# Products of 1024 columns from double banks, one ring for ScalarE's banks, and output chains that share a bank with the sums

## The chip, the cores and the metric

The kernel runs on one core of a Trainium2 chip. The metric is device microseconds of the whole program, median of several executions; executions of one kernel mostly agree within 0.7%. An execution that is more than 1.5% above the fastest of its kernel counts as slow, the others as fast. Each kernel was run beside executions of the kernel before on the same chip; the medians of those lie between 771.1 and 775.0 us, so that times of different rounds can be set side by side to about 4 us, and 1 to 3 us between them are not to be read closely. "Slot" below is one step of the kernel's steady loop. "Clock" is TensorE's granted clock as the profile records it, 1.0 for full and 0.5 for half.

## The reference

Two parts, joined. The first pools x (4 batches of 12416 tokens of 128 channels) into 32 inducing vectors h by softmax attention, then lets each token attend to the 32 h. The second is a gated layer with 1536 hidden units:

```python
def mab(q, kv):
    s = scale * (q @ kv.transpose(0, 2, 1))
    s = s - s.max(-1, keepdims=True)
    a = np.exp(s)
    a /= a.sum(-1, keepdims=True) + 1e-09
    return a @ kv
h = mab(I, x)                     # I: the inducing vectors, per batch
x1 = mab(x, h)                    # per token, over 32 h
...
gate = np.maximum(x1 @ w_gate, 0.0)
val = x1 @ w_val
return (gate * val @ w_out)
```

## The kernel before

The second attention is never formed. Its unnormalised weights p2 (32 rows per token block) are multiplied straight with hgv = h @ w_gate and h @ w_val, so each hidden block needs only matmuls with 32 rows (K = 32), and the squared softmax sum (z2) is divided out at the end. A pair of token blocks (2 x 512 tokens) takes twelve slots, one for each 128 of the 1536 hidden units:

```python
for k in range(2):                 # TensorE, slot `at`
    if k < len(unit):
        form(unit[k], 0)           # g_k of this slot, into a g bank (ring of 3)
    if k < len(before):
        form(before[k], 1)         # v_k of the slot before, into a v bank (ring of 3)
...                                # planned ScalarE/VectorE/DMA work of other parts
for _ in range(steps.pop(at, 0)):
    out_step(at)                   # output chain: o += wo[i] x gv[i], 12 steps, one o bank
for f in fill.pop(at, []):
    f()                            # s2, z2, s1T, hgv, h ... into one "m" bank
for t in unit:
    nc.scalar.activation(out=g16, in_=t["ps", 0], func=AF.Relu)
for t in before:
    nc.vector.tensor_tensor(out=t["dst"], in0=t["g16"], in1=t["ps", 1], op=ALU.mult)
```

(Allocation of g16 is cut. s2 and z2 are the scores and the softmax sums of the second attention, s1T the scores of the first.) The four forms of a slot are placed on four different row groups of the array and run together: in the kernel before three of them start at 112.38 us and the fourth at 112.51, each 0.37 to 0.39 us long. A chain of twelve 128x128x512 matmuls per token block follows, planned as

```python
plan_chain(base + 10 + 6 * k, (2, 2, 2, 3, 3), ...)
```

that is 2, 2, 2, 3, 3 steps in five slots and one slot of pause, in which ScalarE empties the o bank. The kernel's eight PSUM banks are g 3, v 3, m 1, o 1.

The softmax here doesn't subtract the row's maximum and nothing guards it: scores larger than these inputs give would overflow.

Of the kernel before, what the change touches and what calls it, by code (L numbers as in the profile page):

```python
# [17 lines left out]
def kernel(  # L18
# [39 lines left out]
    def bank(tag, name, shape=None, dtype=FP32):  # L58
        return psum.tile(
            shape or [P, BLK], dtype, tag=tag, bufs=3 if tag in ("g", "v") else 1, name=name  # L60
        )
# [61 lines left out]
    def new_xT(q):  # L123
        t0, t1 = crange(q)
        return st([P, t1 - t0, P], FP16, "xT" if t1 - t0 == CT else "xTr", 10 if t1 - t0 == CT else 2)
# [14 lines left out]
    def hgv_pe(hT, k, tag="m"):  # L140
        ps = bank(tag, "hgv_ps")
        for r in range(4):
            nc.tensor.matmul(
                ps[32 * r : 32 * r + 32, :],
                hT[:, 0:M],
                (wg if r % 2 == 0 else wv)[:, k * BLK : (k + 1) * BLK],
                start=True,
                stop=True,
            )
        return ps  # L150

    def hgv_evac(hgv, ps, k):
        if k % 2 == 0:
            nc.scalar.copy(out=hgv[:, k * BLK : (k + 1) * BLK], in_=ps)
        else:
            nc.vector.tensor_copy(out=hgv[:, k * BLK : (k + 1) * BLK], in_=ps)
# [5 lines left out]
    def s2_pe(hT, xT, pr):  # L162
        ps = bank("m", "s2_ps")
# [10 lines left out]
    def s2_exp(ps, pr):  # L174
        p2 = st([P, BLK], FP16, "p2", 3)
        if pr < NPAIR:
            nc.scalar.activation(out=p2, in_=ps, func=AF.Exp, scale=sm_scale)  # L177
        else:
            nc.scalar.activation(out=p2[0:64, 0:P], in_=ps[0:64, 0:P], func=AF.Exp, scale=sm_scale)
        return p2  # L180

    def z2_pe(p2, pr):
        ps = bank("m", "z2_ps", [P, TPB, 2], FP32)
        if pr < NPAIR:
            for t in range(TPB):
                nc.tensor.matmul(ps[:, t, :], p2[:, t * P : (t + 1) * P], sel, start=True, stop=True)  # L186
        else:
            nc.tensor.matmul(ps[:, 0, 0:1], p2[0:64, 0:P], sel[0:64, 0:1], start=True, stop=True)
        return ps

    def z2_recip(ps, pr):
        z2i = st([P, TPB, 2], FP32, "z2i", 4)
        if pr < NPAIR:
            nc.vector.reciprocal(out=z2i, in_=ps)
        else:
            nc.vector.reciprocal(out=z2i[:, 0, 0:1], in_=ps[:, 0, 0:1])
        return z2i
# [5 lines left out]
    hT_ps = bank("o", "hT_ps", [P, M], FP32)  # L203
    z1_ps = bank("m", "z1_ps", [P, CT, M], FP32)
# [17 lines left out]
    for q in range(NCH):  # L222
# [16 lines left out]
        for a in range(t0, t1, 8):  # L239
            e = min(a + 8, t1)  # L240
            ps = bank("g" if a == t0 else "v", "xT_ps", [P, 8, P], FP16)
# [10 lines left out]
        ps = bank("g" if q % 2 else "v", "s1_ps", [P, CT, M], FP32)  # L252
# [11 lines left out]
    pss = [hgv_pe(hT, k, "g") for k in range(3)]  # L264
# [28 lines left out]
    def ev_z2(b, pr, at):  # L293
        def pe():
            ps = z2_pe(p2s[(b, pr)], pr)

            def dve():
                z2is[(b, pr)] = z2_recip(ps, pr)

            post[at + 1].append(dve)  # L300

        fill[at].append(pe)

    for b in range(B):
        for pr in range(NPAIR + 1):
            if (b, pr) == (0, 0):
                ev_z2(0, 0, 1)
            elif pr == 0:
                base = slot(b - 1, NPAIR - 1, 0)
                ev_s2(b, 0, base + 9)  # L310
                ev_z2(b, 0, base + 12)
            else:
                base = slot(b, pr - 1, 0)
                ev_s2(b, pr, base + 3)
                ev_z2(b, pr, base + 6)


    def plan_phase1(b):
# [11 lines left out]
        for q in range(NCH):  # L330
# [17 lines left out]
            at = at0 + NFF * q  # L348
# [4 lines left out]
            def s1(q=q, at=at + 21):  # L353
                ps = bank("m", "s1T_ps")
# [25 lines left out]
            if q < NQ:  # L380
                fill[at + 21].append(s1)

        at = at0 + NFF * NCH + 9

        def s1_rest(at=at):
            ps = bank("m", "s1T_ps")
# [23 lines left out]
        at = at0 + NFF * (NQ + 2) + 8  # L410

        def h_part(q):
            if q == 0:
                s["h_ps"] = bank("m", "h_ps", [P, P], FP32)
# [16 lines left out]
        for q, d in enumerate((0, 1, 1, 2, 3, 4, 5)):  # L431
            fill[at + d].append(lambda q=q: h_part(q))

        def sums():
# [8 lines left out]
        post[at + 6].append(sums)  # L443

        def join():
            ps = bank("m", "hz_ps", [P, 2, M], FP32)
# [3 lines left out]
            def dve():  # L450
                s["hT"] = finish_h(ps[:, 0, :], ps[:, 1, :])
                s["hgv"] = new_hgv()

            post[at + 13].append(dve)

        fill[at + 12].append(join)
        for k in range(3):

            def mk(k=k, a=at + 13 + 2 * k):
                ps = hgv_pe(s["hT"], k)  # L460
                post[a + 1].append(lambda: hgv_evac(s["hgv"], ps, k))

            fill[at + 13 + 2 * k].append(mk)
# [5 lines left out]
    chains = []  # L469

    def out_step(at):

        c = chains[0]
        i = c["i"]
        w = c["w"]
        if i == 0:
            c["ps"] = bank("o", "o_ps")
        nc.tensor.matmul(  # L478
            c["ps"][:, 0:w], wo[:, i, :], c["gv"](i), start=(i == 0), stop=(i == NFF - 1)
        )  # L480
        c["i"] += 1
        if c["i"] < NFF:
            return
        chains.pop(0)
        ps, nt = c["ps"], w // P

        def evac():
            oT = st([P, BLK], FP16, "oT", 3)
            nc.scalar.copy(out=oT[:, 0:w], in_=ps[:, 0:w])  # L489

            def tr():
# [3 lines left out]
                def scale():  # L495
                    osb = st([P, TPB, P], FP32, "osb", 3)
                    z = z2is[c["key"]]
                    for t in range(nt):
                        zz = z[:, t, c["k"] : c["k"] + 1]
# [9 lines left out]
                    def store():  # L509
                        nc.sync.dma_start(  # L510
                            out=ov[c["b"]][:, c["t0"] : c["t0"] + nt, :], in_=osb[:, 0:nt, :]
                        )

                    post[at + 5].append(store)

                post[at + 3].append(scale)

            post[at + 2].append(tr)

        post[at + 1].append(evac)  # L520

    steps = defaultdict(int)

    def plan_chain(first, counts, **c):
        chains.append(dict(i=0, **c))
        for d, n in enumerate(counts):
            steps[first + d] += n
# [3 lines left out]
    def units():  # L531
        for b in range(B):
            for pr in range(NPAIR + 1):
                base = slot(b, pr, 0)
                p2, hgv = p2s[(b, pr)], state[b]["hgv"]
                if pr < NPAIR:
                    gvs = [st([P, NFF, BLK], FP16, "gv", 5) for _ in range(2)]
                    for k in range(2):
                        plan_chain(
                            base + 10 + 6 * k,  # L540
                            (2, 2, 2, 3, 3),
                            w=BLK,
                            gv=(lambda i, g=gvs[k]: g[:, i, :]),
                            key=(b, pr),
                            k=k,
                            b=b,
                            t0=(2 * pr + k) * TPB,
                        )
                    for s in range(NFF):
                        yield [  # L550
                            dict(
                                mm=[
                                    [(slice(0, BLK), s, p2[r : r + 32, :], hgv[r : r + 32, :])]
                                    for r in (64 * k, 64 * k + 32)
                                ],
                                dst=gvs[k][:, s, :],
                            )
                            for k in range(2)
                        ]
                else:  # L560
                    gv = st([P, NFF, P], FP16, "gvr", 1)
                    plan_chain(
                        base + 10,
                        (6, 6),
                        w=P,
                        gv=(lambda i, g=gv: g[:, i, :]),
                        key=(b, pr),
                        k=0,
                        b=b,
                        t0=NT - 1,  # L570
                    )
                    for s in range(3):
                        yield [
                            dict(
                                mm=[
                                    [
                                        (
                                            slice(i * P, (i + 1) * P),
                                            4 * s + i,
                                            p2[r : r + 32, 0:P],  # L580
                                            hgv[r : r + 32, :],
                                        )
                                        for i in range(4)
                                    ]
                                    for r in (0, 32)
                                ],
                                dst=gv[:, 4 * s : 4 * s + 4, :].rearrange("p i c -> p (i c)"),
                            )
                        ]

    def form(t, j):
        ps = t["ps", j] = bank("gv"[j], "gv"[j] + "_ps")
        for cols, s, p2, hgv in t["mm"][j]:
            nc.tensor.matmul(ps[:, cols], hgv[:, s * P : (s + 1) * P], p2, start=True, stop=True)  # L594

    at = 0
    todo_units = units()
    before = []
# [52 lines left out]
```

## Time and profile before

The median is 773.9 us. What matters of the profile:

| | kernel before |
|---|---|
| span of the profiled execution | 771.5 us |
| VectorE busy, 110 to 700 us | 98.9% |
| VectorE idle before its products | 7.0 us |
| ScalarE idle before its relus | 40.2 us |
| mean clock | 0.971 |

How the rows are read stands in the prediction.

### The profile page before, as it was taken

The numbers are of one execution on the slowest core, as the hardware profiler recorded it, in microseconds if no ns is written. First come the engines' busy times: TensorE is split into PE (matmuls) and PEld (weight loads), VectorE is DVE, ScalarE is ACT, GpSimd is POOL, SyncE is SP. The second block draws the span as 40 slices with busy tenths as digits, with TensorE's granted clock in tenths as the row PEclk, the third lists the DMA queues.
The fourth block names the chain that finished last, engine by engine and source line by source line (L and its number), as shares of the span: only waits on it lengthen the run. The fifth ranks groups of instructions, "written<-read, shape, count | busy, mean of one in ns | idle before, by whom it ended". The sixth has DMA issues, their size and how long they took to land.

```text
span 771.5 us, 15512 instructions
## 1 busy us (share of the span) xinstructions
PE 709.3 (92%) x4621; PEld 210.3 (27%) x4621; DVE 722.4 (94%) x1270; ACT 695.4 (90%) x1386; POOL 207.2 (27%) x418
## 2 busy tenths in 40 slices
PE   5699999999999999999999999999999999999993
PEld 4422222232232222222222222223222222222221
DVE  3399999999999999999999999999999999999991
ACT  4589999999989999999998999999989999999991
POOL 0303433221232243122123323322122212212212
PEclk9759999999999999999998999999999999999998
DMA  8635675211136756312134676421121121121122
GB/s 312 199 83 135 158 190 124 69 57 49 55 119 150 202 141 163 87 58 51 52 117 128 151 184 172 102 64 47 55 57 53 50 62 55 49 63 56 49 62 60
DMA packets 121172, 78.87 MB, mean 102 GB/s; under 512 B 102880, under 2 KB 105472, under 8 KB 118016
## 3 DMA queue, kind: packets, MB, share of 16 engines
q1 hardware_dynamic: 121088, 77.89, 37.3%
q8 instruction: 36, 0.59, 0.3%
q14 instruction: 48, 0.39, 0.2%
HBM read 27.80 MB, written 25.43 MB: 69 GB/s over the span
## 4 chain that ended last, share of the span: by engine, by line
PE 51%; ACT 20%; issue 12%; DMA 8%; DVE 4%; POOL 3%; SPq 0%; ACTq 0%; POOLq 0%; DVEq 0%
PE o_ps L478 23%; PE g_ps L594 18%; ACT g L616 14%; PE v_ps L594 7%; DMA xT<-x 3%; DVE gv L618 3%; DMA o<-oT 3%; ACT oT L489 3%; POOL osb L500 2%; ACT p L177 1%; POOL x L337 1%; ACT p1T L367 1%; PE xT_ps L243 1%; DMA p1g<-p1T 1%; PE h_ps L423 1%
## 5 line engine op out<-in xcount | busy, mean ns | idle before, releaser
L618 DVE TENSOR_TENSOR gv<-g,v_ps 128x512 f16<-128x512 f16 x1152 | 696.2, 679 | 7.0 <-PE v_ps L594 5.8
L616 ACT ACTIVATE g<-g_ps 128x512 f16<-128x512 f32 x1164 | 615.6, 626 | 40.2 <-PE g_ps L594 20.1
L594 PE MATMUL v_ps<-p,hgv 32*128 32x512 f16 (+1 forms) x1200 | 368.3, 381 | 4.7 <-DVE gv L618 2.8
L478 PE MATMUL o_ps<-gv,wo 128*128 128x512 f16 x1152 | 336.6, 389 | 0.3 <-ACT oT L489 0.3
L594 PE MATMUL g_ps<-p,hgv 32*128 32x512 f16 (+1 forms) x1200 | 303.3, 381 | 28.8 <-ACT g L616 26.5
L500 POOL TENSOR_SCALAR osb<-o,z2i 128x128 f32<-128x128 f16 x388 | 168.0, 447 | 527.6 <-DMA o<-oT 310.9
L594 PEld LDWEIGHTS <-hgv 32*128 32x128 f16 x2400 | 91.0, 91 | 287.6 <-issue 276.4
L478 PEld LDWEIGHTS <-wo 128*128 128x128 f16 x1200 | 76.9, 98 | 189.4 <-issue 164.9
L489 ACT CAST oT<-o_ps 128x512 f16<-128x512 f32 (+1 forms) x100 | 58.5, 585 | 4.4 <-PE o_ps L478 4.4
L337 POOL CAST x<-x 128x2048 f16<-128x2048 f32 x18 | 34.0, 1890 | 5.3 <-DMA x<-in_x_dram 5.3
L177 ACT ACTIVATE p<-s_ps 128x512 f16<-128x512 f32 x48 | 30.8, 641 | 2.7 <-PE s_ps L167 2.6
L167 PE MATMUL s_ps<-xT,hT 128*64 128x512 f16 x96 | 20.0, 413 | 1.6 <-DVE hT L137 1.6
L243 PE MATMUL xT_ps<-eye,x 128*128 128x128 f16 x97 | 11.1, 287 | 8.1 <-ACT x L227 4.4
L245 DVE COPY xT<-xT_ps 128x1024 f16<-128x1024 f16 x6 | 4.2, 692 | 13.7 <-PE xT_ps L243 13.7
L186 PEld LDWEIGHTS <-p 128*128 128x128 f16 x192 | 11.5, 97 | 12.4 <-issue 2.3
L247 ACT COPY xT<-xT_ps 128x1024 f16<-128x1024 f16 x6 | 6.1, 1012 | 6.4 <-PE xT_ps L243 6.4
L186 PE MATMUL z_ps<-sel,p 128*128 128x2 f16 x192 | 11.7, 165 | 0.0
L367 ACT ACTIVATE p1T<-s1T_ps 128x512 f16<-128x512 f32 x18 | 11.6, 645 | 0.0
L243 PEld LDWEIGHTS <-x 128*128 128x128 f16 x97 | 8.5, 130 | 9.4 <-ACT x L227 5.7
L167 PEld LDWEIGHTS <-hT 128*64 128x64 f16 x96 | 5.3, 107 | 20.1 <-issue 18.4
L618 DVE TENSOR_TENSOR gvr<-g,v_ps 128x512 f16<-128x512 f16 x12 | 8.1, 674 | 2.2 <-PE g_ps L594 1.2
L227 ACT CAST x<-x 128x1024 f16<-128x1024 f32 x6 | 6.2, 1038 | 4.0 <-DMA x<-in_x_dram 4.0
(74 smaller groups left out, 112.7 us busy)
## 6 DMA issues: line engine op xcount, KB each, us to landing
x<-in_x_dram SPq DMA_DIRECT2D x24, 1024.0 KB, 5.7
out_dram<-osb SPq DMA_DIRECT2D x96, 256.0 KB, 2.0
o<-oT SPq DMA_TRANSPOSE x100, 2.4
x<-in_moe_w_gate_dram SPq DMA_DIRECT2D x1, 768.0 KB, 4.3
x<-in_moe_w_val_dram SPq DMA_DIRECT2D x1, 768.0 KB, 4.3
x<-in_moe_w_out_dram SPq DMA_DIRECT2D x1, 768.0 KB, 6.1
xT<-x SPq DMA_TRANSPOSE x18, 4.3
p1g<-p1T SPq DMA_TRANSPOSE x18, 2.9
```

What stands on the lines that cost most here:

```text
L167: nc.tensor.matmul(ps[64 * k : 64 * k + 64, :], hT, xTs(xT, t0, TPB), start=True, stop=True)
L177: nc.scalar.activation(out=p2, in_=ps, func=AF.Exp, scale=sm_scale)
L186: nc.tensor.matmul(ps[:, t, :], p2[:, t * P : (t + 1) * P], sel, start=True, stop=True)
L243: nc.tensor.transpose(ps[:, t - a, :], x16[:, t, :], eye16)
L337: nc.gpsimd.tensor_copy(out=s["x16"][:, t0:t1, :], in_=s["x32", q])
L367: nc.scalar.activation(out=p1T, in_=ps, func=AF.Exp, scale=sm_scale, accum_out=s["zp"][:, q : q + 1])
L478: nc.tensor.matmul(c["ps"][:, 0:w], wo[:, i, :], c["gv"](i), start=(i == 0), stop=(i == NFF - 1))
L489: nc.scalar.copy(out=oT[:, 0:w], in_=ps[:, 0:w])
L500: nc.gpsimd.tensor_scalar(out=osb[:, t, :], in0=o16[:, t, :], scalar1=zz, scalar2=zz, op0=ALU.mult, op1=ALU.mult,)
L594: nc.tensor.matmul(ps[:, cols], hgv[:, s * P : (s + 1) * P], p2, start=True, stop=True)
L616: nc.scalar.activation(out=g16, in_=t["ps", 0], func=AF.Relu)
L618: nc.vector.tensor_tensor(out=t["dst"], in0=t["g16"], in1=t["ps", 1], op=ALU.mult)
```

## The change

The intent: one product of 1024 columns costs VectorE less than two of 512 (0.066 us a slot less by my estimate), so multiply both token blocks of a slot at once. For that the two v banks lie side by side (a double bank, two of them, four banks in place of three); the kernel stays at eight, so the m bank is given up. What ScalarE empties besides the relus (s2, s1T, hgv) goes through the ring of three g banks. What VectorE empties (z2, h and its join) becomes a "job" in the one o bank, and chains and jobs take turns there, in order, three steps a slot. The core of the diff, cut:

```diff
-            shape or [P, BLK], dtype, tag=tag, bufs=3 if tag in ("g", "v") else 1, name=name
+            shape or [P, BLK], dtype, tag=tag, bufs={"g": 3, "v": 2, "o": 1}[tag], name=name
...
-        ps = bank("m", "s2_ps")
+        ps = bank("g", "s2_ps")
...
-    def z2_pe(p2, pr):
-        ps = bank("m", "z2_ps", [P, TPB, 2], FP32)
+    def z2_pe(p2s):
+        ps = bank("o", "z2_ps", [P, 2, TPB, 2], FP32)
...
+            before["v"] = bank("v", "v_ps", [P, 2 * BLK])
...
+        h = (len(gs) + 1) // 2
+        for f, m in gs[:h] + vs + gs[h:]:          # forms in the order g0, v0, v1, g1
+            f(*m)
...
+        budget = 3.0 if unit else 100.0
+        while jobs and free <= at and budget > 0:
+            j = jobs[0]
+            when, cost, f = j["steps"][0]
+            if when > at:
+                break
+            f()
+            budget -= cost
+            j["steps"].pop(0)
+            if not j["steps"]:
+                jobs.pop(0)
+                free = at + 2                      # one slot in which the bank is emptied
...
-        for t in before:
-            nc.vector.tensor_tensor(out=t["dst"], in0=t["g16"], in1=t["ps", 1], op=ALU.mult)
+            nc.vector.tensor_tensor(
+                out=before["dst"], in0=before["g16"][:, 0:n], in1=before["v"][:, 0:n], op=ALU.mult
+            )
```

Other parts: the z2 sums of two pairs come at once, hgv is emptied by ScalarE alone, and the next batch's first phase is spread over 16 slots a chunk in place of 12.

## The prediction

> **What bounds the kernel now.** I read the page's busy shares first, then the groups of instructions, then the waits of the stretch 110 to 700 us, and last the order of single instructions on VectorE, ScalarE and TensorE. The work is a pipeline of 588 slots: 576 in which two units of 512 columns are formed (TensorE: four row-tile matmuls into g and v banks), passed through relu on ScalarE, and multiplied on VectorE, plus 12 short slots for the left-over tokens. Output chains (o, 24 matmuls per 12 slots) and small fills share TensorE.
>
> The page, busy time and groups:
> ```profile
> PE 709.3 (92%) x4621; PEld 210.3 (27%) x4621; DVE 722.4 (94%) x1270; ACT 695.4 (90%) x1386; POOL 207.2 (27%) x418
> ...
> L618 DVE TENSOR_TENSOR gv<-g,v_ps 128x512 f16<-128x512 f16 x1152 | 696.2, 679 | 7.0 <-PE v_ps L594 5.8
> L616 ACT ACTIVATE g<-g_ps 128x512 f16<-128x512 f32 x1164 | 615.6, 626 | 40.2 <-PE g_ps L594 20.1
> ```
> Three engines look close, but the idle column parts them: VectorE waits 7.0 us before its 1152 products, ScalarE 40.2 us before its relus. The same by stretch, where 110 to 700 us is the steady part:
> ```profile
> 110.00:700.00 590.00, 560.37 (x3587) 159.04 (x3586) 583.31 (x1021) 555.22 (x1120) 162.53 (x335) 0.99 0.36 94
> ```
> Columns: PE, PEld, DVE, ACT, POOL, granted clock. VectorE is busy 583.31 of 590, 98.9%; it is the bound. TensorE's 95% is not a rate: matmuls overlap[...]. The chain of waits gives PE 51%, but it follows single releases, and on a pipeline whose VectorE has 1% idle I trust the idle time instead.
>
> VectorE in order of time (start, length):
> ```profile
> 119.64 13.88 DVE L618 TENSOR_TENSOR gv<-g,v_ps 128x512 f16<-128x512 f16 x23
> 133.44 0.20 DVE L194 RECIPROCAL z2i<-z_ps 128x8 f32<-128x8 f32 x1
> 133.56 6.64 DVE L618 TENSOR_TENSOR gv<-g,v_ps 128x512 f16<-128x512 f16 x11
> ```
> 23 products start every (133.44-119.64)/23 = 0.600 us, though one lasts 0.679: neighbours overlap by 0.08. The small reciprocal holds the queue only 0.12 us.
>
> ScalarE in order of time:
> ```profile
> 113.77 0.59 ACT L489 CAST oT<-o_ps 128x512 f16<-128x512 f32 x1
> 114.23 1.12 ACT L616 ACTIVATE g<-g_ps 128x512 f16<-128x512 f32 x2
> 115.20 0.65 ACT L177 ACTIVATE p<-s_ps 128x512 f16<-128x512 f32 x1
> 115.67 4.14 ACT L616 ACTIVATE g<-g_ps 128x512 f16<-128x512 f32 x8
> ```
> Fed without a gap, a relu costs (115.20-114.23)/2 = 0.485 us, an oT cast 0.46, an exp 0.47.
>
> TensorE in order of time, one slot with three chain steps:
> ```profile
> 112.38 0.38 PE L594 MATMUL g_ps<-p,hgv 32*128 32x512 f16 x1
> 112.38 0.39 PE L594 MATMUL v_ps<-p,hgv 32*128 32x512 f16 x1
> 112.38 0.38 PE L594 MATMUL g_ps<-p,hgv 32*128 32x512 f16 x1
> 112.51 0.37 PE L594 MATMUL v_ps<-p,hgv 32*128 32x512 f16 x1
> 112.82 0.82 PE L478 MATMUL o_ps<-gv,wo 128*128 128x512 f16 x3
> 113.57 0.38 PE L594 MATMUL g_ps<-p,hgv 32*128 32x512 f16 x1
> ```
> The four form matmuls run together; from the last of them to the first chain step 0.31 us; three steps and the way back 0.75. The slot is 1.19 us, of which 0.13 is the late fourth form.
>
> [...]
>
> **The change part by part.**
> 1. *One product of 1024 columns in place of two of 512.*[...] It saves 0.066 x 576 = 38.0 us of VectorE, all on the bound.
> 2. *Reciprocals for two pairs at once:* 48 become 24, each 0.12 us of queue: 2.9 us. *All hgv evacuations on ScalarE:* four VectorE casts go, some 0.6 each: 2.4 us. VectorE sheds 43 us in all. From its first product (39.6 us) to its last (756.6) it needs 717 us now; it would need about 674.
> 3. *ScalarE keeps its relus at 512* and gains four casts. Its minimum: 1164 x 0.485 = 565; oT 100 x 0.46 = 46; exps 48 x 0.47 = 23; phase-one exps with their accumulator reads 18 x 0.57 = 10; hgv 12 x 0.46 = 6. Sum 650 us. That fits in 674, at 96%, where today it has 91%. So VectorE stays the bound, with ScalarE 4% behind.
> 4. *TensorE does the same matmuls.* Two chain steps a slot on average: forms 0.31, steps 2 x 0.22[...], fills some 0.1: an estimated 0.95 us against a slot of 1.15. But the schedule gives three steps a slot for four slots and then a pause (chains must leave the one o bank for a slot). Such slots take 1.06 to 1.19, at or above the new 1.134, and the pause returns it.
> 5. *Banks.* g keeps 3 single banks but now also takes s2, s1T and hgv; v has 2 double banks, 4 in place of 3; the old m bank goes. A double v bank frees once per slot. Forms of v need some 0.45 us and are wanted a full product (1.13) later, so the ring of two holds if TensorE isn't late by over half a slot. Each fill put into the g ring brings its own ScalarE instruction of 0.47, which gives TensorE that time back.
> 6. *Start and end.* The first 39 us and the last 15 (last chain, transposing DMA, scaling, store) hold nearly the same work; 0 to 1 us more at the end, as z2 and the chains now queue for one bank. DMA is 36% busy in the steady part and no product waits on it by name; moving phase one from 12 to 16 slots a chunk spreads it.
>
> Sum: 773.9 - 43 = 731 us if VectorE stays as full as now. I add 12 us for the tighter coupling (below) and come to 743.
>
> **Rivals.**
> - *ScalarE and TensorE take the bound between them.* With 4% spare, ScalarE can no longer absorb its 40 us of waiting for g banks filled late. For it: of its steady idle time 26 us is on TensorE, and TensorE waits 22.6 us on ScalarE for g banks: that loop of 3 banks is already taut. Against it: those waits partly exist because VectorE holds TensorE back. If half of the 40 us stayed, ScalarE would need 670 us, VectorE's own figure[...]: 745 to 757 us.
> - *Chain steps that catch up with the products.* After z2 a chain of an even pair starts close behind the units it reads; some 8 of 24 slots have a step that reads the product just issued, now available only when all 1024 columns are done. TensorE, in order, then sits 0.3 to 0.8 us before the next forms. My slack there is about 0.2 us. At 0.1 us lost in each of 190 such slots: 19 us, so about 750. If it loses 0.2, the gain is gone to within 2%.
> - *The per-instruction 0.067 us is hidden in the old rhythm* (say the wait for the other engine's signal is what shows between products). Then 1024 columns cost nearly 1.20 and only part 2 remains: 768 us. Against it: the rhythm is the same 0.600 in stretches with and without slack elsewhere.
> - *Nothing is lost:* 731 to 735.
>
> **Range and chances.** The middle is 743. The floor is part 1 and 2 in full, 731. The upper end adds one of the first two rivals nearly in full, 758. Faster by over 2% needs below 758.4; that fails only if more than 60% of the 43 us is given back, which I put at 0.14, with 0.03 for a slowdown by serialised start-up banks or a stalled joint bank.
>
> **What would show it.** Step 1: products of 128x1024 starting 1.13 to 1.14 us apart when back to back, lasting about 1.21; 576 of them. Step 2: 24 reciprocals of 128x16; no hgv cast on VectorE. Step 3: relus again 0.485 apart; ScalarE's idle time before them cut from 40 to some 20 us, its share at 93 to 95%. If VectorE's busy share of the steady part falls below 95% and its waits name v_ps or g_ps, a rival has come true: g banks if ScalarE is fuller than 96%, chain steps if TensorE's chain line shows waits on VectorE's product, which now has none. A product over 1.17 us back to back would make step 1 wrong.

The forecast's sum: 38.0 + 2.9 + 2.4 = 43 us off 773.9, so 731, and 743 with 12 us for coupling. In part 1 the 1.134 us for a product of 1024 columns, the 0.066 us a slot (38.0 us) and the 0.067 us per instruction were my estimate. The two traces have shown since that products with no idle time between them start 0.598 us apart at 512 columns (median of 1067, kernel before) and 1.132 apart at 1024 (median of 330, changed kernel): 2 x 0.598 - 1.132 = 0.064 us, 37 us in 576 slots. In part 4 an item of 0.1 is cut, so what is left there adds up to 0.85 of the 0.95; the trace shows it as 0.31 us from the last form to the first chain step against some 0.22 from one step to the next (three take 0.82, one 0.38). The first rival's 745 to 757 rested on an estimate of what two full engines cost each other, which was not shown.

## More of the kernel before

The mean clock got no attention in the prediction. It should have: 0.971 means that (1 - 0.971) x 2 x 771.5 = 45 us ran at half clock, which lay at the start, the end and two of the three batch boundaries.

## The result

The changed kernel takes 806.1 us (805.0 to 806.9, four executions) against 773.8 for the kernel before. The ratio is 1.043, 95% interval 1.038 to 1.047: slower. Ratios here are the mean time of one kernel's fast executions over that of the other's in the same rounds, so they are not quite the ratios of the medians. The time lies far outside the predicted 731 to 758.

From the page of the changed kernel, busy time and groups:
```profile
PE 717.5 (89%) x4621; PEld 207.6 (26%) x4621; DVE 698.5 (87%) x666; ACT 707.2 (88%) x1390; POOL 207.6 (26%) x418
...
L651 DVE TENSOR_TENSOR gv<-g,v_ps 128x1024 f16<-128x1024 f16 x576 | 674.4, 1214 | 68.7 <-PE g_ps L591 37.9
L648 ACT ACTIVATE g<-g_ps 128x512 f16<-128x512 f32 x1164 | 616.3, 621 | 45.2 <-PE g_ps L591 36.9
L481 PE MATMUL o_ps<-gv,wo 128*128 128x512 f16 x1152 | 354.0, 417 | 14.0 <-DVE gv L651 13.7
```
The products are there, 576 of them at 1.214 us. But VectorE now idles 68.7 us before them, ten times what it did, and the releaser named for most of it, 37.9 us, is TensorE. ScalarE waits 45.2 us, 36.9 of it for TensorE. And one and the same chain matmul takes 417 ns on average, where it took 389 in the kernel before:
```profile
L478 PE MATMUL o_ps<-gv,wo 128*128 128x512 f16 x1152 | 336.6, 389 | 0.3 <-ACT oT L489 0.3
```

Why a matmul got longer is in the row of the granted clock, 40 slices of the span. First the kernel before, then the changed one:
```profile
PEclk9759999999999999999998999999999999999998
```
```profile
PEclk9779999998988899899897989998898899998998
```
Before, the clock dips at the start, once near the middle and at the end. Now it dips in many slices, and the mean is 0.901: (1 - 0.901) x 2 x 805 = 159 us at half clock against 45.

What comes before a dip shows when the trace is cut along the recorded clock changes, which in this trace come 3.41 us or a multiple of it apart (half clock lasts 3.41, 6.83 or 10.24 us between 55 and 740 us). The next view gives the busy time and count of the chain matmuls alone, changed kernel, in four such windows (columns: stretch, length, PE busy and count, PEld busy and count, clock, DMA share, GB/s):
```profile
133.59:137.00 3.41, 2.38 (x9) 0.55 (x9) 1.00 0.56 105
137.00:140.42 3.42, 0.19 (x1) 0.11 (x2) 1.00 0.42 117
140.42:143.83 3.41, 2.59 (x6) 0.43 (x4) 0.50 0.89 301
143.83:147.24 3.41, 1.64 (x6) 0.42 (x6) 1.00 0.31 102
```
Nine chain matmuls, then one, then a window at half clock, then full clock again. The same view of the kernel before shows an even load:
```profile
122.45:125.86 3.41, 1.82 (x6) 0.34 (x6) 1.00 0.43 120
125.86:129.28 3.42, 1.64 (x6) 0.42 (x6) 1.00 1.02 191
```
The window with one chain matmul is no idle window. In order of time it holds forms and the z2 sums; TensorE is recorded as busy for 87% of it. From the order of time of the changed kernel, around it:
```profile
138.27 0.35 PE L184 MATMUL z_ps<-sel,p 128*128 128x2 f16 x8
...
140.23 1.32 PE L481 MATMUL o_ps<-gv,wo 128*128 128x512 f16 x3
...
142.03 1.46 PE L481 MATMUL o_ps<-gv,wo 128*128 128x512 f16 x3
...
142.24 1.22 DVE L651 TENSOR_TENSOR gv<-g,v_ps 128x1024 f16<-128x1024 f16 x1 [0.21 <-PE g_ps L591]
```
The z2 slot lies between two pauses, so three slots, some 3.4 us, pass without a chain step. After them three chain steps take 1.32 and 1.46 us, where they took 0.82 at full clock, and VectorE waits.

I counted this over the whole changed trace (55 to 740 us): for each window at full clock, how many 512-column matmuls with all 128 rows (chain steps and s2) start in it, and whether the next window is at half clock.

| full-row matmuls in the window | windows | next window at half clock |
|---|---|---|
| 0 to 3 | 35 | 24 |
| 4 or more | 127 | 0 |

In all, 38 windows there ran at half clock; in the kernel before, 4.

This count is a sign and not a rule. Eleven of the 35 windows were not followed by half clock, and over the traces of all fifteen kernels, with fillers counted too, 117 of 257 windows with three such matmuls or fewer were, and 8 of 2546 with more. A finer count nearly separates them: take of each matmul the part of the array that it uses (rows x columns of its shape on the page, as 32*128, over the largest there, 128*128) and the time that its columns take (216 ns for 512, the median spacing of chain steps at full clock in the changed kernel), and add this up as a share of the window.

| share of the array in use, windows at full clock | changed kernel: windows, next at half | all fifteen kernels: windows, next at half |
|---|---|---|
| under 0.35 | 22, 22 | 100, 99 |
| 0.35 to 0.40 | 8, 2 | 87, 26 |
| 0.40 and more | 132, 0 | 2616, 0 |

By this count a form is worth a quarter of a chain step, s2 half of one, and the z2 sums next to nothing: the window from 137.00 has a share of 0.25 although TensorE is recorded as busy for 87% of it. The count was made after all the runs and on kernels of one family, so it describes them; no run was planned to test it.

The clock isn't all. This is the changed kernel's TensorE at full clock:
```profile
130.75 0.37 PE L591 MATMUL g_ps<-p,hgv 32*128 32x512 f16 x1
131.15 0.39 PE L591 MATMUL v_ps<-p,hgv 32*128 32x512 f16 x2
131.73 0.37 PE L591 MATMUL g_ps<-p,hgv 32*128 32x512 f16 x1 [0.20 <-ACT g L648]
132.03 0.82 PE L481 MATMUL o_ps<-gv,wo 128*128 128x512 f16 x3
132.79 0.41 PE L164 MATMUL s_ps<-xT,hT 128*64 128x512 f16 x2
133.13 0.38 PE L591 MATMUL g_ps<-p,hgv 32*128 32x512 f16 x1
```
This follows a pause. In the pause TensorE can't get ahead: its next form waits for a g bank that a relu must free (the 0.20). Then come three chain steps and s2, and the next forms start 1.40 us after the last one (133.13 - 131.73), above the 1.13 us at which VectorE's products start back to back in this trace. VectorE waits 0.24 us for it.

### The profile page after: what moved, and what is told of

Its sections match the earlier page's. It is cut to its first block, busy times and chain, and to the rows that moved or that the text cites. A ratio compares the mean times of both kernels' runs of the same rounds, so it can differ in the third digit from the quotient of the medians.

```text
span 805.1 us, 13705 instructions
## 1 busy us (share of the span) xinstructions
PE 717.5 (89%) x4621; PEld 207.6 (26%) x4621; DVE 698.5 (87%) x666; ACT 707.2 (88%) x1390; POOL 207.6 (26%) x418
## 4 chain that ended last, share of the span: by engine, by line
PE 56%; ACT 24%; issue 10%; DVE 8%; DMA 2%; POOL 0%; SPq 0%; POOLq 0%; ACTq 0%; DVEq 0%
PE o_ps L481 28%; PE g_ps L591 19%; ACT g L648 17%; DVE gv L651 8%; ACT oT L487 5%; PE v_ps L591 3%; PE s_ps L164 2%; DMA o<-oT 1%; PE xTb_ps L239 1%; DMA x<-in_x_dram 1%; PE h_ps L431 1%; PE hgv_ps L143 1%; ACT x L223 1%; PE s1T_ps L367 1%; ACT p L251 0%
## 5 line engine op out<-in xcount | busy, mean ns | idle before, releaser
L651 DVE TENSOR_TENSOR gv<-g,v_ps 128x1024 f16<-128x1024 f16 x576 | 674.4, 1214 | 68.7 <-PE g_ps L591 37.9
L648 ACT ACTIVATE g<-g_ps 128x512 f16<-128x512 f32 x1164 | 616.3, 621 | 45.2 <-PE g_ps L591 36.9
L481 PE MATMUL o_ps<-gv,wo 128*128 128x512 f16 x1152 | 354.0, 417 | 14.0 <-DVE gv L651 13.7
L591 PE MATMUL g_ps<-p,hgv 32*128 32x512 f16 (+1 forms) x1200 | 318.2, 401 | 41.8 <-ACT g L648 29.4
L591 PE MATMUL v_ps<-p,hgv 32*128 32x512 f16 (+1 forms) x1200 | 245.2, 404 | 6.1 <-DVE gv L651 5.8
L591 PEld LDWEIGHTS <-hgv 32*128 32x128 f16 x2400 | 77.8, 92 | 281.0 <-issue 276.5
L481 PEld LDWEIGHTS <-wo 128*128 128x128 f16 x1200 | 90.3, 102 | 215.7 <-issue 176.8
L243 ACT COPY xT<-xTb_ps 128x1024 f16<-128x1024 f16 x6 | 6.1, 1012 | 6.8 <-PE xTb_ps L239 6.8
L184 PEld LDWEIGHTS <-p 128*128 128x128 f16 x192 | 6.5, 97 | 21.4 <-issue 21.4
L153 ACT CAST hgv<-hgv_ps 128x512 f16<-128x512 f32 x12 | 6.9, 596 | 2.9 <-PE hgv_ps L143 2.7
L239 PE MATMUL xTb_ps<-eye,x 128*128 128x128 f16 x48 | 5.8, 295 | 4.1 <-ACT x L223 4.1
```

The costliest lines, as they stand in the source:

```text
L239: nc.tensor.transpose(ps[:, t - a, :], x16[:, t, :], eye16)
L481: nc.tensor.matmul(c["ps"][:, 0:w], wo[:, i, :], gv(i), start=(i == 0), stop=(i == NFF - 1))
L591: nc.tensor.matmul(ps[:, cols], hgv[:, s * P : (s + 1) * P], p2, start=True, stop=True)
L648: nc.scalar.activation(out=g16[:, k * BLK : (k + 1) * BLK], in_=ps, func=AF.Relu)
L651: nc.vector.tensor_tensor(out=before["dst"], in0=before["g16"][:, 0:n], in1=before["v"][:, 0:n], op=ALU.mult)
```

## The experiments

Thirteen kernels ran, all of them correct.

**1. A filler in the z2 slot (warm_z2).** If the hole of three slots halves the clock, then more work there should make the kernel faster.

```diff
             before["v"] = bank("v", "v_ps", [P, 2 * BLK])
+            if jobs and jobs[0].get("z2") and free <= at and jobs[0]["steps"][0][0] <= at:   # z2 runs here
+                for _ in range(3):       # overwritten by the forms of v
+                    nc.tensor.matmul(before["v"][:, 0:BLK], wo[:, 0, :], wg[:, 0:BLK],
+                                     start=True, stop=True)
```

> The changed kernel, plus three throw-away 128x128x512 matmuls in each slot in which the z2 sums run (some 27 slots, written into the v bank before its own forms; the result stays right). Theory 1 (clock): the pause, the z2 slot and the next pause leave 3.4 us without a full-array matmul, and TensorE's granted clock then falls to half for 3.4 us or more; it stood at half for (1-0.901)x2x805 = 159 us against 45 before. With the filler the granted clock returns to 0.96 or more and the time falls to 770 to 785 although TensorE does 17 us more work. Theory 2 (bursts: three chain steps a slot behind a ring of three g banks): the loss is elsewhere, the time stays at 800 to 815, whatever the clock does.

Measured: 784.3 us, clock 0.953, 13 half-clock windows in place of 38. That is 22 us faster for doing more. Between the two profiled executions, in which the windows were counted, it is 24.5 us (806.9 to 782.3), about 1 us for each window that went. VectorE's idle time fell accordingly (page, the group of products):
```profile
L657 DVE TENSOR_TENSOR gv<-g,v_ps 128x1024 f16<-128x1024 f16 x576 | 670.1, 1213 | 46.9 <-PE g_ps L592 22.4
```
The clock is a cause. It isn't the only one, for 46.9 us of idle time stay. The number fell in the range of theory 1, the clock itself a little short of it.

**2. The z2 sums in the g ring (z2_in_g).** The hole shrinks to one slot without any added work.

```diff
-        ps = bank("o", "z2_ps", [P, 2, TPB, 2], FP32)
+        ps = bank("g", "z2_ps", [P, 2, TPB, 2], FP32)
...
-        job([(base + (6 if pr < NPAIR else 0), 3, pe)], dve)
+        fill[at].append(both)            # at = slot(b, pr, 6); reciprocal one slot later
```

> The changed kernel with the z2 sums in the ring of g banks, not as a job in the one o bank: the hole of three slots without chain steps becomes one slot, nothing is added. Theory 1 (clock): granted clock 0.96 or more, 768 to 780 us. Theory 2 (bursts): still four slots of three steps and a pause, and one more user of the g ring: 795 to 810.

Measured: 795.2 us, clock 0.936, 22 half-clock windows. Theory 1 (768 to 780) missed by 15 us or more; the time lies at the edge of theory 2's range, 795 to 810. The schedule and the trace show why: without z2 the chains catch up with the products sooner and then run at one step a slot, and one step a slot beside a pause also leaves windows with three full-row matmuls or fewer. TensorE's wait for products before its chain steps rose from 13.7 to 45.0 us (page):
```profile
L486 PE MATMUL o_ps<-gv,wo 128*128 128x512 f16 x1152 | 350.9, 405 | 45.4 <-DVE gv L656 45.0
```

**3. The product undone, the rest kept (split_product).**

```diff
-            nc.vector.tensor_tensor(out=before["dst"], in0=..., in1=before["v"][:, 0:n], op=ALU.mult)
+            for a in range(0, n, BLK):
+                nc.vector.tensor_tensor(out=before["dst"][:, a : a + BLK], ...)
```

> The changed kernel with each product of 1024 columns undone into two of 512, banks and schedule kept. It puts back 38 us of VectorE work. Theories 1 and 2: TensorE sets the pace, VectorE idles 69 us before its products, so nearly all of the 38 us is absorbed: 803 to 818, clock 0.90. Rival (coarse products are the cause: chain steps and bank releases come only when all 1024 columns are done): the time falls, to under 795.

Measured: 809.3 us, clock 0.899. The double product is worth 3 us in this schedule, no more than rounds differ by, and coarse products are not the cause of the loss.

**4. Chains spread as before (even_chains).** z2 in the g ring as in 2, and each chain planned at the slots of the kernel before.

```diff
+                        jobs[-1]["plan"] = base + 10 + 6 * k
...
+            # step n of a chain not before slot start + slow[n]
+            slow = (0, 0, 1, 1, 2, 2, 3, 3, 3, 4, 4, 4)
+            d = j["n"] // 3 if j["late"] else slow[j["n"]]     # late: three a slot, as in the change
+            if at < j["start"] + d:
+                break
```

> z2 sums in the g ring, and the chains of each pair spread as in the kernel before: 2, 2, 2, 3, 3 steps and a pause in place of 3, 3, 3, 3 and a pause. Theories 1 and 2 together: clock 0.97, VectorE over 96% busy in the steady part, 735 to 752 us. If only the clock mattered (1 without 2): the same as z2_in_g to within 5 us. If the g ring shared with s2, s1T, hgv and z2 is what holds it (ring): 760 or more with ScalarE waiting on g_ps.

Measured: 754.5 us (753.7 to 755.1), ratio to the kernel before 0.977, interval 0.974 to 0.980. It is faster than both kernels, with the double products, the double v banks and the shared g ring all in place. It lies 2.5 us above the expected range. From its page, and its steady part (PE, PEld, DVE, ACT, POOL, clock):
```profile
L668 DVE TENSOR_TENSOR gv<-g,v_ps 128x1024 f16<-128x1024 f16 x576 | 665.4, 1213 | 24.6 <-ACT g L665 9.8
L665 ACT ACTIVATE g<-g_ps 128x512 f16<-128x512 f32 x1164 | 608.6, 629 | 24.0 <-PE g_ps L597 16.6
L486 PE MATMUL o_ps<-gv,wo 128*128 128x512 f16 x1152 | 332.6, 388 | 0.4 <-ACT oT L492 0.4
```
```profile
110.00:700.00 590.00, 542.50 (x3656) 154.10 (x3655) 569.84 (x537) 565.85 (x1149) 167.90 (x341) 0.99 0.37 97
```
VectorE is 96.6% busy, the clock in the steady part is back at 0.99, and a chain matmul is back at 388 ns. VectorE's idle time is 24.6 us; the largest part of it, 9.8 us, is now put down to ScalarE, which is busy 95.9%.

**5. The kernel before with the changed kernel's chain timing (before_bursts).** One part of the change alone.

```diff
-                            base + 10 + 6 * k,
-                            (2, 2, 2, 3, 3),
+                            base + (15 if k else 8 if pr % 2 else 10),
+                            (3, 3, 3, 1, 1, 1) if pr % 2 and k == 0 else (3, 3, 3, 3),
```

> The kernel before, with only the timing of its output chains changed to that of the changed kernel: per two pairs 3, 3, 3, 3, pause, 3, 3, 3, 3, pause, 3, 3, 3, 1, 1, 1, pause, 3, 3, 3, 3 and then three slots without chain steps. Products, banks and everything else as before. Theory 1 (the hole throttles TensorE's clock): granted clock 0.90 to 0.93 in place of 0.97, some 25 half-clock stretches, 790 to 805 us. Rival (the double v bank and the shared g ring are needed for the loss): 770 to 780 us, clock 0.96 or more.

Measured: 834.0 us median; three executions (832.5 to 836.1, clock 0.89) count as slow because the fourth took 818.9 (clock 0.921). So there is no interval, and only the fast one may be compared: 818.9 against 770.6 to 775.1. The profile, from a slow execution, has 41 half-clock windows. The chain timing alone, with single banks, a bank for fills and products of 512, costs 43 us or more in the one execution that may be compared, which is more than the whole change does. The rival, that double banks and the shared ring are needed for the loss, is out.

**6. Filler in every slot short of chain steps (warm_all).** In the changed kernel, two throw-away matmuls in a slot without a chain step, one in a slot with one.

```diff
+            full = peek(at)              # chain steps that will run in this slot
+            for _ in range(max(0, 2 - full) if at > 12 else 0):
+                nc.tensor.matmul(before["v"][:, 0:BLK], wo[:, 0, :], wg[:, 0:BLK], ...)
```

> The changed kernel, its timing kept, with throw-away 128x128x512 matmuls so that every slot has at least two full-array matmuls (two in a slot without a chain step, one in a slot with one). Theory 1: granted clock 0.965 or more, under 8 half-clock windows in place of 38; from the trace of the changed kernel, its half-clock and mixed slots cost some 34 us over full-clock ones, so 768 to 778 us. What stays above 754 us (chains spread evenly) is then the cost of the bursts (theory 2), some 20 us. If the two theories are one and the clock is all: 752 to 760.

Measured: 780.8 us, clock 0.982, no half-clock window between 55 and 740 us; 3 us above the expected range. With the clock full all along, 26 us remain above the evenly spread chains. Part of these is the filler itself, as run 11 shows, so the number is an upper bound for what the timing costs at full clock.

**7. Filler for the even kernel (even_warm).** Two throw-away matmuls in the second and later of chain-less slots in a row (`range(2 if quiet > 1 and at > 12 else 0)`), on top of run 4.

> The kernel with z2 in the g ring and evenly spread chains (754.5 us), plus two throw-away matmuls in every second or later chain-less slot in a row, which are those at the batch boundaries. Five half-clock windows were left there; at some 0.9 us each: 748 to 753 us, clock 0.97 to 0.98. If it is slower than 755 the filler costs more than the clock gives.

Measured: 753.7 us, clock 0.982, no half-clock window left in that stretch; just above the expected 748 to 753. One microsecond, so the five windows that were left cost hardly more than their filler.

**8. Order of the forms (even_order).** `gs[:h] + vs + gs[h:]` replaced by g0, v0, g1, v1 on top of run 4.

> Evenly spread chains with z2 in the g ring, and the forms of a slot in the order g0, v0, g1, v1 of the kernel before, in place of g0, v0, v1, g1. If the wait of g1 for its bank is what delays v and so VectorE, the new order is slower, by up to 8 us; if the order doesn't matter: 751 to 758.

Measured: 763.0 us, clock 0.961. The order of the change, with g1 last, is worth 8.5 us here (7 by the ratios). The other order puts v1 behind g1, which waits for a bank that a relu must free (in run 4 TensorE's g forms waited 26.7 us for relus between 110 and 700 us). It also had ten half-clock windows, in place of five, so a part of the 8.5 may be the clock's.

**9. Bursts with a filler (burst_warm).** Run 4 with `slow = (0, 0, 0, 1, 1, 1, 2, 2, 2, 3, 3, 3)`, so four slots of three steps and two of pause, and two throw-away matmuls in each chain-less slot.

> The evenly spread kernel (z2 in the g ring) with its chains back at 3, 3, 3, 3 steps and two slots of pause, started where the even ones start (so hardly a step reads a product just issued), and two throw-away matmuls in every chain-less slot, which keeps the clock full (0.975 or more). If it is the bursts that cost what is left of the loss at full clock (27 us between 781 and 754): 768 to 782. If it was rather the chain steps that catch up with the products, or z2 as a job of the o bank, that cost it: 752 to 760.

Measured: 779.8 us, clock 0.979. I read that at first as the cost of bursts at full clock. Runs 11 and 12 take that reading back.

**10. The product undone in the even kernel (even_split).** The edit of run 3 on top of run 4.

> The evenly spread kernel (z2 in the g ring) with each product of 1024 columns undone into two of 512. If the step of the prediction that 1024-column products save VectorE 0.066 us a slot, 38 us, is right and on the path there: 780 to 792. If little of it is on the path: 756 to 768.

Measured: 770.7 us, ratio to the kernel before 0.996. The double product is worth 16.2 us there (15 by the ratios), which lies between the two ranges that I expected, nearer to "little". With single products VectorE is the bound again (its group of products, page, and the steady part):
```profile
L669 DVE TENSOR_TENSOR gv<-g,v_ps 128x512 f16<-128x512 f16 x1152 | 692.9, 676 | 14.1 <-PE g_ps L597 6.5
```
```profile
110.00:700.00 590.00, 543.16 (x3578) 159.23 (x3576) 578.70 (x996) 556.94 (x1122) 164.18 (x335) 0.98 0.37 96
```
98.1% busy against 96.6% with double products. So the saving is real, but less than half of the predicted 38 us reaches the kernel's time.

**11. Control for the filler (even_fill).** Run 4 with four throw-away matmuls in each slot without a chain step, which is mostly its one pause slot per chain.

> Control for the filler: the evenly spread kernel with four throw-away matmuls in its one pause slot per chain, 16 per two pairs, as many as in the kernel of bursts with a filler. If the filler costs little: 752 to 759, and the 26 us between bursts with filler (779.8) and even chains with filler (753.7) belong to the bursts. If the filler itself is what costs: 765 or more.

Measured: 813.6 us, clock 0.983 with no half-clock window from 55 to 740 us. So a filler is not free, even in a pause slot: the kernel is 59 us longer than run 4. It is not quite the control that it was meant to be, for the trace has 476 throw-away matmuls against 386 in run 9, and four in a slot in place of two. In order of time:
```profile
283.95 1.02 PE L656 MATMUL v_ps<-wg,wo 128*128 128x512 f16 x4
...
284.91 0.39 PE L598 MATMUL g_ps<-p,hgv 32*128 32x512 f16 x1
...
285.44 2.35 DVE L699 TENSOR_TENSOR gv<-g,v_ps 128x1024 f16<-128x1024 f16 x2 [0.41 <-PE g_ps L598]
```
The four matmuls push the forms of that slot back, and VectorE waits 0.41 us for them. The slots around it, with two steps each, are short, but don't give it back: VectorE's idle time before its products is 78.7 us, against 24.6 in run 4. That TensorE can't run far enough ahead with these banks is my reading of it.

**12. Bursts without a filler (burst_cold).** Run 9 without its throw-away matmuls.

> The kernel of bursts (3, 3, 3, 3 and two slots of pause, z2 in the g ring) without the throw-away matmuls. Theory 1: the windows with three full-array matmuls or fewer throttle the clock, 0.91 to 0.95, 790 to 810 us, and the difference to 779.8 is the clock's. If two slots of pause aren't enough to throttle: 772 to 782, clock 0.965 or more.

Measured: 781.6 us, clock 0.944, 16 half-clock windows. Two slots of pause do throttle, less often than expected. The time equals that of run 9: what the filler gave back of the clock it took in its own time. So run 9 doesn't tell bursts and clock apart. The comparison without fillers does: 781.6 against 754.5, 27 us for bursts in place of even chains at otherwise equal work. It also bounds what the catching-up costs. In this kernel TensorE does not wait for a product before a chain step (page):
```profile
L486 PE MATMUL o_ps<-gv,wo 128*128 128x512 f16 x1152 | 337.0, 400 | 0.4
```
It is 13.6 us faster (12 by the ratios) than run 2 (795.2), the other kernel with z2 in the g ring, whose chains catch up (45.0 us). Part of that is the clock's, 0.943 against 0.928 as means of the executions, and the pauses differ too, so no more than that is shown.

**13. The batch boundary (even_h).** Run 4 with the h sums of the next batch in one slot and a g bank, so that they don't delay the chains.

```diff
-                s["h_ps"] = bank("o", "h_ps", [P, P], FP32)
+                s["h_ps"] = bank("g", "h_ps", [P, P], FP32)
...
-        s["jobs"] = [...]
+        fill[at].append(h_all)
+        fill[at + 3].append(hz)
```

> The evenly spread kernel with the h sums of the next batch all in one slot, in a g bank, and their join in another, so that the chains no longer fall eight slots behind at a batch boundary and catch up at three steps a slot. Removes about eight late chains at each of three boundaries: at 0.6 us each 14 us, less some 2 us for the long slot, so 742 to 750. If the held g bank stalls the ring: 752 to 760.

Measured: 752.4 us (751.5 to 753.8), ratio 0.973, interval 0.969 to 0.976; clock 0.981. It is the fastest kernel. The gain over run 4 is 2 us, within what rounds differ by, not the 4 to 12 expected: late chains cost less than I thought, or the held bank took it back. That isn't settled.

**Slots by clock.** From the traces, each interval from one product's start to the next (before: from one slot's first product to the next), by the mean recorded clock in it: full above 0.99, half below 0.55, mixed else.

| kernel | full: count, mean us | half | mixed |
|---|---|---|---|
| before | 552, 1.237 | 19, 1.403 | 4, 1.478 |
| changed | 463, 1.245 | 68, 1.590 | 44, 1.495 |
| burst_cold | 519, 1.226 | 30, 1.618 | 26, 1.609 |
| even_chains | 548, 1.207 | 21, 1.253 | 6, 1.843 |

From the changed kernel to even_chains, the clock's share is the excess of half and mixed slots over full ones: 68 x 0.345 + 44 x 0.250 = 34.5 us, less 21 x 0.046 + 6 x 0.636 = 4.8 us in even_chains, so 29.7. The share at full clock is (1.245 - 1.207) x 575 = 21.9. The sum, 51.6, is no check of this split: the intervals add up to the time from the first product to the last, whatever the clock did. The split is an estimate, for the slots at half clock are also those just after a hole, which may be long for other reasons. Runs 1 and 6, which removed 25 and 38 half-clock windows and became 22 and 25 us faster with their fillers, show that the clock's share is large. Of the 27 us of run 12, by the same sum, the clock has about 17 and the bursts at full clock (1.226 - 1.207) x 575 = 11.

## Why the prediction was wrong

**Step 1, the product, was right in its pace, and off the path.** A product lasts 1.214 us (predicted about 1.21), and in the even kernel eleven of them in a row take 12.62 us, (12.62 - 1.21)/10 = 1.14 apart. But in the changed schedule it isn't VectorE that sets the pace: undoing it costs 3 us (run 3). Where the chains are even, it is worth 16 us of the predicted 38 (run 10). Between runs 10 and 4 the time that VectorE is recorded in products fell by 27.5 us (692.9 to 665.4) and its idle time before them rose by 10.5 (14.1 to 24.6), which leaves 17. A product that starts after a wait doesn't overlap the one before it, as those in a row do (1.21 us long, 1.14 apart), so a part of what is missing from 38 is waiting as well.

**Step 2 was right in kind.** A reciprocal for two pairs holds VectorE's queue longer than the 0.12 us assumed, 0.16 (139.58 to the product at 139.74), so some 2 us are saved in place of 2.9. The groups of the changed kernel by shape have:
```profile
L153 ACT CAST hgv<-hgv_ps 128x512 f16<-128x512 f32 x12 | 6.9, 596 | 2.9 <-PE hgv_ps L143 2.7
...
L306 DVE RECIPROCAL z2i<-z_ps 128x16 f32<-128x16 f32 x24 | 6.0, 250 | 0.0
```

**Step 3 holds for the even kernel only.** ScalarE's waits before relus were to fall from 40 to 20 us: 45.2 in the changed kernel, 24.0 in even_chains, at 95.9% busy in the steady part.

**Step 4 failed, in two places.** "Such slots take 1.06 to 1.19, at or above the new 1.134, and the pause returns it." The slots were sized about right where only chain steps run (1.13 and 1.17 us after 133.13), but with s2 in it such a slot took 1.40, and the pause does not return it: run 11 shows that a slot made longer is paid by VectorE although short ones stand beside it, and the order of time at 131 us shows TensorE held in a pause by a g bank. In place of slots of 1.13 to 1.15 us the changed kernel has slots of 1.245 us at full clock and of 1.59 at half. And the step took TensorE's rate as given. It treated chain steps only as a load, never as what keeps the clock up. The hole of three slots at the z2 job was in the schedule that the diff spells out, and the granted clock was on the page of the kernel before, with its dips at the batch boundaries, where the chains thin out. In the changed kernel's record the clock changes come 3.41 us or a multiple apart, from 1.0 to 0.5 and back. TensorE need not stand idle for it: in the 24 full-clock windows that half clock followed it was recorded as busy for 70 to 88% (for 87% in the window from 137.00). I had not asked what lowers the clock of a kernel whose TensorE is busy for 95% of the steady part, and that was the costliest omission: some 30 us of the 63 between 743 and 806.

**The middle of 743 assumed 12 us for coupling.** Even at its best timing the design ends at 752 to 754, 21 to 23 us above the floor of 731, so that term was about twice as large. Mis-sized, not wrong.

**The rivals.** "Chain steps that catch up with the products" came true in part: TensorE waits 13.7 us for products before chain steps, where it had no such wait, and runs 2 and 12 differ by 13.6 us, not all of it for this. "ScalarE and TensorE take the bound between them" is the state of the even kernel. "The fixed cost is hidden" is out, by run 10 (16.2 us) and by the 0.064 us a slot of the traces. The one that decided, a lower clock, wasn't on the list. The prediction's signs would not have told either: VectorE's busy share of the steady part did fall below 95% (536.56 of 590 us, 90.9%) with g_ps named, but ScalarE was not fuller than 96% (537.87 us, 91.2%). A chance of 0.03 for slower was too sure for a change that also rewrote the timing of half of TensorE's work.

What stays open: what decides between shares of the array of 0.35 and 0.40, where 26 of 87 windows were followed by half clock, and how much of the 22 us at full clock is the z2 job's place and how much is the catching-up. Run 12 bounds only the bursts.

## What to carry to other kernels

Read a schedule change for what it takes away from TensorE in any 3.4 us, not only for what it adds: on this kernel three slots without chain steps mostly cost half the clock for 3.4 us or more (after 24 of 35 windows with three full-row matmuls or fewer), though small matmuls kept TensorE "busy". Here the share of the array in use told it: under 0.35 in a window of 3.41 us the clock went to half 99 times in 100, at 0.40 and more never in 2616. That is a count over the traces, not a rule. With rings of two and three banks, spread the filler work of an engine evenly, for here a long slot was paid at once and the short ones beside it didn't give it back (run 11: VectorE idle for 78.7 us against 24.6). And when a bundle of edits is slower, try its parts on the old timing before dropping it: with the chains spread evenly, the same banks and products beat the old kernel by 2.3 to 2.8%.
